# V of 24-bit precision in two float16 parts with a common power of two, and work moved between the vector engines, in a fused block-causal attention and gated convolution FFN

## The chip, the cores and the metric

The kernel runs on one core of a Trainium2 chip. Such a core has a matrix engine (TensorE, PE in the profile, with its weight loads shown apart as PEld), three engines for elementwise work (VectorE = DVE, ScalarE = ACT, GpSimd = POOL) and SyncE (SP), which here only starts data transfers. Each engine works through its own list of instructions in order and waits at semaphores for the others. [...]

The metric is the device time of one execution in microseconds (us).

## The reference

```python
# q, k, v: (8 batches, 8 heads, 576 positions, 64);  w_in (512, 1024), conv_w (3, 1024), w_out (1024, 512)
scores = scale * np.matmul(q, k.transpose(0, 1, 3, 2))          # scale = 1/8
scores = np.where(block_i >= block_j, scores, -1000000000.0)    # blocks of 64 positions
scores = scores - np.max(scores, axis=-1, keepdims=True)
attn = np.exp(scores)
attn = attn / (np.sum(attn, axis=-1, keepdims=True) + 1e-09)
attn_out = np.matmul(attn, v)
...
h = np.maximum(x @ w_in, 0.0)                                   # x: the heads side by side, (8, 576, 512)
conv_out = sum over k of conv_w[k] * h shifted by k - 1 along the sequence
out = (h * sigmoid(conv_out)) @ w_out
```

The weights arrive as float64 and are decoded on the chip. Everything is computed to nearly float32 precision: most factors are split into a high part and a low remainder, and each matrix product is made of three products (high x high, high x low, low x high).

## The kernel before

**Stages.** The work goes by pairs of heads; two heads of 64 channels fill the 128 partitions. The first batch (four pairs) is handled in two halves, A (positions 0 to 255) and B (the rest), with code of its own, so that the weights can be decoded beside it. The other 28 pairs go through `stage_t` (q and k are transposed on PE and split), `stage_s` (scores, mask, maximum, exponential, division, planes), a transposition of the planes, and `pair_pv`. After the fourth pair of a batch, `ffn` runs on its two halves. Its matrix products (L1887 into the hidden layer, L1953 out of it) are interleaved with the attention of the next batch.

**Planes.** Before the change `two_planes` splits each tile of normalized exponentials, scaled by 32768, into two float16 planes: the high one on GpSimd (L1366), the low one on VectorE (L1371). Query tile i (0 to 3) has 128 (i + 1) keys, and the last 64 queries (`last_s`) have 576, in two halves of 288. SP then issues one transposing transfer for each plane of each head (`xbar`, L1379, ten blocks of 128 x 128), and one more for the last queries' planes (`h` to `t`).

**V.** `load_v` splits V into three bfloat16 parts on GpSimd: copy, subtract, copy, subtract, each 640 wide. `pair_pv` then makes five products (parts 0, 1, 2 with the high plane, parts 0, 1 with the low one), in one burst for the queries 0 to 255 (4 multiplications a product) and one for the queries 256 to 575 (18 a product), all at L1844: 110 multiplications a pair.

**FFN.** For each chunk of 128 hidden channels `ffn` makes 12 multiplications into a PSUM bank (L1887), then a chain: rectify in place on ACT (L1901), middle tap on ACT into a buffer `t` (L1904), the two other taps on DVE (L1908, L1912), hyperbolic tangent on ACT (L1917), gate on DVE (L1920, the last reader of the bank), high part `gh` on ACT (L1924), low part `gl` on GpSimd (L1927). The output tiles are copied on ACT (L1961) and stored by SP (L1964).

**What sets the order.** Nothing is scheduled while the kernel runs. `Plan.order` lists every operation with an engine, an estimated duration and a target time from the table `TARGETS`, and lays the operations out engine by engine, by target among those whose inputs are ready by its estimates; it also hands out the PSUM banks. Where it expects PE to stand still it puts idle multiplications (`work`, L2078), which keep PE busy and give nothing. Each transfer takes the next of eight semaphores, and so waits until the transfer that used this semaphore last has landed (`DMAHW` in the rows below).

**The start.** `load_first` loads q and k of the first 256 positions of all heads in six pieces each, pairs 0, 1 and 2 to 3, into one buffer `qkt`; `first_t` transposes them pair by pair (L1319).

Of the kernel before, what the change touches and what calls it, by code (L numbers as in the profile page):

```python
# [349 lines left out]
class Plan:  # L350

    DRAIN = (0.165, 0.08, 0.1, 0.025, 0.0)
    SIGNAL = (0.04, 0.035, 0.035, 0.08, 0.1)
# [1758 lines left out]
```

## Time and profile before

| | before |
|---|---|
| median of 3 runs (lowest, highest) | 769.39 us (767.01, 769.42) |
| the profiled execution | 767.56 us |
| its span, first to last instruction | 765.6 us |
| busy: PE, DVE, ACT, POOL | 728.7, 634.3, 491.7, 447.5 us |
| mean granted clock of TensorE | 0.993 |

A row of a group reads: line, engine, operation, output <- inputs by the program's names, shape, count | busy time in us, mean ns of one | idle time of the engine just before them, and who ended it. In the timeline a row gives the start, the duration, the group, and in brackets the idle time before it and who ended it. Multiplications are pipelined, so their durations overlap, and the distance of the starts is what each costs. A row of waits reads: who waited <- for whom: us in total, times, longest us. SPq and ACTq are the queues of transfers that SP and ACT issue; issuing is not counted as busy time.

### The profile page before, as it was taken

Reading aid. Unit: us, or ns where it says so; the run is one execution under the profiler, and the core shown is the slowest. Engines: PE = TensorE matmul, PEld = TensorE weight load, DVE = VectorE, ACT = ScalarE, POOL = GpSimd, SP = SyncE. Lnnn points to the kernel's source line nnn. Section 1 sums busy time; section 2 is a strip of 40 time slices with the busy share of each in tenths; the row PEclk is TensorE's granted clock in tenths of the full one; section 3 lists DMA queues with packets and bytes.
Section 4 is the critical chain, followed back from the end, with each engine's and each line's share of the span. In section 5 each row is a group of like instructions: output and inputs, shape, how many; then the busy total and the mean of one; then the engine's idle time right before and its main releaser. Section 6 shows DMA issues by size and latency. Waiting matters only on the chain.

```text
span 765.6 us, 19659 instructions
## 1 busy us (share of the span) xinstructions
PE 728.7 (95%) x7028; PEld 617.5 (81%) x7028; DVE 634.3 (83%) x1749; ACT 491.7 (64%) x1466; POOL 447.5 (58%) x604
## 2 busy tenths in 40 slices
PE   5989999799999999999999999999989999999998
PEld 3656678686878879888988889788878888888987
DVE  0888899898999889899998888999878977996442
ACT  1788977655766648676765548576655746673654
POOL 0353476667667757475668655686745864673232
PEclk9999999999999999999999999999989999999999
DMA  5564446669858498376858468796749548665001
GB/s 155 139 191 117 110 108 131 118 128 179 166 101 172 92 161 161 86 162 136 155 93 176 98 136 144 126 181 116 151 86 154 126 98 157 123 115 87 29 28 42
DMA packets 323061, 96.35 MB, mean 126 GB/s; under 512 B 312316, under 2 KB 317460, under 8 KB 322964
## 3 DMA queue, kind: packets, MB, share of 16 engines
q1 hardware_dynamic: 322420, 94.97, 61.9%
q8 instruction: 56, 0.92, 0.5%
q14 instruction: 41, 0.34, 0.1%
q10 hardware_dynamic: 544, 0.13, 0.1%
HBM read 37.38 MB, written 9.44 MB: 61 GB/s over the span
## 4 chain that ended last, share of the span: by engine, by line
PE 60%; DVE 19%; DMA 8%; ACT 6%; issue 3%; POOL 1%; SPq 1%; ACTq 0%; POOLq 0%; DVEq 0%
PE bank L1953 21%; PE bank L1887 16%; PE bank L1844 10%; PE bank L1477 5%; DVE ptbl L1371 3%; DVE su L1493 3%; DMA t<-h 3%; PE bank L1400 2%; PE bank L1268 2%; DVE t L1908 2%; DVE t L1912 1%; DVE t L1920 1%; DMA ptbh<-ptbl 1%; DMA x<-in_moe_w_out_dram 1%; DVE su L1504 1%
## 5 line engine op out<-in xcount | busy, mean ns | idle before, releaser
L1887 PE MATMUL bank<-x,wih 128*128 128x290 f32 (+3 forms) x1024 | 193.5, 300 | 2.1 <-DVE t L1920 0.9
L1927 POOL TENSOR_TENSOR gl<-t,gh 128x289 fp32r<-128x289 f32 (+3 forms) x128 | 108.5, 855 | 107.6 <-ACT gh L1924 107.2
L1887 PEld LDWEIGHTS bank<-x,wih 128*128 128x128 f32 x1024 | 153.9, 188 | 10.1 <-issue 3.1
L1953 PE MATMUL bank<-woh,gh 128*128 128x512 f32 (+1 forms) x296 | 120.0, 406 | 1.0 <-POOL ptbl L1366 1.0
L1953 PE MATMUL bank<-wol,gh 128*128 128x512 f32 (+1 forms) x296 | 114.7, 388 | 0.0
L1953 PE MATMUL bank<-woh,gl 128*128 128x512 f32 (+1 forms) x296 | 114.6, 387 | 0.0
L1887 PE MATMUL bank<-x,wil 128*128 128x290 f32 (+3 forms) x512 | 109.8, 298 | 0.0
L1493 DVE TENSOR_REDUCE su<-bank 128x1 f32<-128x384 f32 (+2 forms) x224 | 100.5, 477 | 3.1 <-ACT p0f L1496 2.1
L1908 DVE SCALAR_TENSOR_TENSOR t<-bank,cw,t 128x289 f32<-128x289 f32 (+3 forms) x128 | 64.0, 506 | 29.9 <-ACT t L1904 29.5
L1887 PEld LDWEIGHTS bank<-x,wil 128*128 128x128 f32 x512 | 81.6, 188 | 2.4 <-issue 1.4
L1917 ACT ACTIVATE t<-t 128x289 f32<-128x289 f32 (+3 forms) x128 | 56.2, 444 | 25.3 <-DVE t L1912 24.8
L1901 ACT ACTIVATE bank<-bank 128x290 f32<-128x290 f32 (+3 forms) x128 | 51.1, 404 | 32.7 <-PE bank L1887 31.9
L1953 PEld LDWEIGHTS bank<-woh,gh 128*128 128x128 f32 x296 | 55.9, 189 | 15.6 <-issue 4.4
L1924 ACT ACTIVATE gh<-t 128x289 fp32r<-128x289 f32 (+3 forms) x128 | 55.0, 442 | 18.4 <-DVE t L1920 17.8
L1904 ACT ACTIVATE t<-bank,cw 128x289 f32<-128x289 f32 (+3 forms) x128 | 63.1, 499 | 4.1 <-POOL gl L1927 1.8
L1953 PEld LDWEIGHTS bank<-woh,gl 128*128 128x128 f32 x296 | 55.9, 189 | 11.9
L1912 DVE SCALAR_TENSOR_TENSOR t<-bank,cw,t 128x288 f32<-128x288 f32 (+3 forms) x128 | 63.5, 505 | 0.5
L1844 PEld LDWEIGHTS <-vx 128*64 128x64 bf16 x1540 | 52.7, 113 | 12.0 <-issue 11.1
L1953 PEld LDWEIGHTS bank<-wol,gh 128*128 128x128 f32 x296 | 56.0, 189 | 7.6
L1920 DVE SCALAR_TENSOR_TENSOR t<-t,bank 128x289 f32<-128x289 f32 (+3 forms) x128 | 56.1, 446 | 5.5 <-ACT t L1917 4.9
L1844 PEld LDWEIGHTS <-vv 128*64 128x64 bf16 x1540 | 50.5, 111 | 6.8 <-issue 6.7
L1844 PE MATMUL bank<-ptbx,vx 128*64 128x256 f16 (+1 forms) x840 | 53.5, 261 | 2.2 <-DMA ptbx<-ptbl 2.0
(189 smaller groups left out, 1757.5 us busy)
## 6 DMA issues: line engine op xcount, KB each, us to landing
out_dram<-stage SPq DMA_DIRECT2D x35, 256.0 KB, 2.5
vn<-in_v_dram SPq DMA_DIRECT2D x58, 128.0 KB, 2.5
...
```

The source lines that it names most:

```text
L1493: nc.vector.tensor_reduce(out=st.ap[:, k:k + 1], in_=sb.ap[:, cols(i)], op=ALU.max, axis=AX.X, negate=True)
L1844: nc.tensor.matmul(tb.ap[64 * j:64 * j + 64, c0:c1], vb.ap[:, j, c, w, :], x, start=first, stop=(w == 1 and z == 1 and c == jobs[-1][0]), ...
L1887: nc.tensor.matmul(fb.ap[:, 0:n2], wt[:, c, fs], xs[c][xi].ap[:, x0:x0 + n2], start=(n + c - c0 == 0), stop=(n + c - c0 == 3 * NCC - 1))
L1901: nc.scalar.activation(out=fb.ap[:, 0:n2], in_=fb.ap[:, 0:n2], func=AF.Relu, scale=0.5)
L1904: nc.scalar.activation(out=t.ap[:, 0:no], in_=fb.ap[:, own:own + no], func=AF.Copy, scale=cw[:, NFC + f:NFC + f + 1])
L1908: nc.vector.scalar_tensor_tensor(out=t.ap[:, i0:no], in0=fb.ap[:, own + i0 - 1:own + no - 1], scalar=cw[:, f:f + 1], in1=t.ap[:, i0:no], o ...
L1912: nc.vector.scalar_tensor_tensor(out=t.ap[:, 0:i1], in0=fb.ap[:, own + 1:own + 1 + i1], scalar=cw[:, 2 * NFC + f:2 * NFC + f + 1], in1=t.a ...
L1917: nc.scalar.activation(out=t.ap[:, 0:no], in_=t.ap[:, 0:no], func=AF.Tanh)
L1920: nc.vector.scalar_tensor_tensor(out=t.ap[:, 0:no], in0=t.ap[:, 0:no], scalar=1.0, in1=fb.ap[:, own:own + no], op0=ALU.add, op1=ALU.mult)
L1924: nc.scalar.activation(out=gbuf[0].ap[:, f, carry:carry + no], in_=t.ap[:, 0:no], func=AF.Copy)
L1927: nc.gpsimd.tensor_tensor(out=gbuf[1].ap[:, f, carry:carry + no], in0=t.ap[:, 0:no], in1=gbuf[0].ap[:, f, carry:carry + no], op=ALU.subtract)
L1953: nc.tensor.matmul(fb.ap[:, 0:cut], gbuf[a].ap[:, f, cs], w[:, f, ds], start=(f == 0 and n == 0), stop=(f == NFC - 1 and n == 2))
```

## The change

- **V.** Each pair's V is multiplied by a power of two so that it fits float16, and split in two float16 parts. ACT sums |V| along each row (a bound for its maximum), GpSimd puts the sums on a diagonal, one multiplication with a matrix of constants spreads them to all partitions, DVE takes the maximum and keeps its exponent bits. GpSimd scales V, copies the high part and subtracts for the low part. `pair_pv` makes three products (66 multiplications), and the copies out of PSUM undo the scale from a per-partition value.
- **Planes.** The planes of both heads lie together in one buffer of 40 blocks, in three pieces: query tiles 0 and 1 with both planes (12 blocks), high plane of tiles 2 and 3 (14), low plane (14). Three transfers take the place of four. The burst of queries 0 to 255 waits for the first piece alone. The 128-key tiles (i = 0) are split on GpSimd alone in three steps; the high planes of the 256-key tiles and of the last queries go to ACT.
- **Masks** are written by ACT instead of DVE. The 64 x 64 corner copies of q that SP made by transfers (L1304) are made by ACT and DVE from PSUM.
- **FFN**, in all batches but the first: the copy `gh` goes to GpSimd, and in chunks 1, 3, 5, 7 the third tap is a product on ACT and an addition on GpSimd.
- **Stores** are issued by ACT, except those of the last half.
- **The start.** `qkt` becomes six buffers, one for each of q and k and each piece.
- The planner counts 0.6 instead of 0.1 us of signalling for SP, some durations are changed, and the table of targets is new.

```diff
@@ planner, constants, first loads
-    SIGNAL = (0.04, 0.035, 0.035, 0.08, 0.1)
+    SIGNAL = (0.04, 0.035, 0.035, 0.08, 0.6)
...
-    HPOOL = (0, 1, 2, 3, 4)
+    HPOOL, HALL = (2, 3), (0,)
+    CPOOL = (1, 3, 5, 7)
+    MACT = True
+    NGRP = ((0, 1), (2,), (3, 4))
...
-    qkt = [nc.alloc_sbuf_tensor_at(f"qk{x}", [P, 2, 2, H, D], d, offset=at0).ap() for x, d in (("f", F32), ("r", F32R))]
+    FIRST = ((0, 1), (1, 2), (2, 4))
+    qkt = [[[nc.alloc_sbuf_tensor_at(f"qk{x}{z}{p0}", [P, 2, 2 * (p1 - p0), D], d, offset=at0 + 4 * D * H * 2 * z + 4 * D * 4 * p0).ap()
+             for p0, p1 in FIRST] for z in range(2)] for x, d in (("f", F32), ("r", F32R))]
@@ load_v
-        def copy(w):
+        def total():
+            nc.scalar.activation(out=piece(1).bitcast(BF16), in_=src(), func=AF.Abs, accum_out=sc.ap[:, 0:1])
+
+        def spread():
+            nc.gpsimd.tensor_scalar(out=dg.ap, in0=ident, scalar1=sc.ap[:, 0:1], scalar2=2.0 ** -100, op0=ALU.mult, op1=ALU.max)
+
+        def all_rows():
+            nc.tensor.matmul(tb.ap[:, 0:P], ones, dg.ap, start=True, stop=True)
+
+        def top():
+            nc.vector.tensor_reduce(out=sc.ap[:, 1:2], in_=tb.ap[:, 0:P], op=ALU.max, axis=AX.X)
+
+        def power(i):
...
-        def less():
-            nc.gpsimd.tensor_tensor(out=src(), in0=src(), in1=piece(0), op=ALU.subtract)
-
-        def last():
-            nc.gpsimd.tensor_tensor(out=piece(2), in0=src(), in1=piece(1), op=ALU.subtract)
+        def level():
+            nc.gpsimd.tensor_scalar(out=src(), in0=src(), scalar1=sc.ap[:, 2:3], scalar2=0.0, op0=ALU.mult, op1=ALU.add)
+
+        def high():
+            pool_copy(piece(0), src())
+
+        def low():
+            nc.gpsimd.tensor_tensor(out=piece(1), in0=src(), in1=piece(0), op=ALU.subtract)
@@ two_planes
+        def even():
+            nc.gpsimd.tensor_scalar(out=tb.ap, in0=tb.ap, scalar1=st.ap[:, col:col + 1], scalar2=0.0, op0=ALU.mult, op1=ALU.add)
+
+        def h1p():
+            pool_copy(hi(), c(tb.ap))
+
+        def h2p():
+            nc.gpsimd.tensor_tensor(out=lo(), in0=c(tb.ap), in1=hi(), op=ALU.subtract)
@@ stage_s
-                    nc.vector.memset(x, MASKED)
+                        if MACT:
+                            nc.scalar.activation(out=x, in_=maskt[0:64, :].unsqueeze(1).broadcast_to([64, len(tiles), 64]), func=AF.Copy)
@@ pair_pv
-                for w, z in ((0, 0), (1, 0), (2, 0), (0, 1), (1, 1)):
+                for w, z in ((0, 0), (1, 0), (0, 1)):
...
-            o = pl.op(PE, (0.77 if qa == 0 else 2.64, 0.05, 0.1), mm, at, deps=deps + [vdone] + (done4 if qa else []),
+            o = pl.op(PE, (0.47 if qa == 0 else 1.65, 0.05, 0.1), mm, at, deps=(deps[1:] + done4 if qa else deps[:1]) + vdone,
@@ ffn
+            def c2u(fb=fb, f=f, u=u):
+                nc.scalar.activation(out=u.ap[:, 0:i1], in_=fb.ap[:, own + 1:own + 1 + i1], func=AF.Copy,
+                                     scale=cw[:, 2 * NFC + f:2 * NFC + f + 1])
+
+            def c2p(t=t, u=u):
+                nc.gpsimd.tensor_tensor(out=t.ap[:, 0:i1], in0=t.ap[:, 0:i1], in1=u.ap[:, 0:i1], op=ALU.add)
...
+            def c5p(t=t, f=f):
+                pool_copy(gbuf[0].ap[:, f, carry:carry + no], t.ap[:, 0:no])
...
-                    nc.sync.dma_start(out=ofl[row:row + P, ds], in_=ob.ap[:, ds])
+                late_ = b == B - 1 and o1 == S
+
+                def st(ob=ob, row=row, ds=ds, eng=nc.sync if late_ else nc.scalar):
+                    eng.dma_start(out=ofl[row:row + P, ds], in_=ob.ap[:, ds])
```

Since the table of targets is new, the instructions stand in another order on every engine. Three places are shown. The first is SP's list at the start of the program, with what each transfer waits for (`qkf` is q and k of the first positions, `gh` and `gl` hold raw `w_in`, `ptbl` raw v). Before:

```order
L1004 DMA qkf<-in_q_dram 128x2x64 x2
L1194 DMA gh<-in_moe_w_in_dram 128x4x256
L1194 DMA gl<-in_moe_w_in_dram 128x4x256 [waits DMAHW0_49]
L1004 DMA qkf<-in_k_dram 128x2x64 [waits DMAHW1_49]
L1004 DMA qkf<-in_k_dram 128x2x64 [waits DMAHW2_49,PE_49]
L1194 DMA gh<-in_moe_w_in_dram 128x4x256 [waits DMAHW3_49]
L1004 DMA qkf<-in_k_dram 128x4x64 [waits DMAHW4_49]
```

And of the change:

```order
L1048 DMA qkf_117<-in_k_dram 128x2x64
L1238 DMA gh<-in_moe_w_in_dram 128x4x256
L1048 DMA qkf_117<-in_k_dram 128x2x64 [waits DMAHW0_49]
L1238 DMA gh<-in_moe_w_in_dram 128x4x256 [waits DMAHW1_49]
L1059 DMA ptbl<-in_v_dram 128x4x64 [waits DMAHW2_49]
L1048 DMA qkf_118<-in_k_dram 128x4x64 [waits DMAHW3_49]
```

The second piece of k for the second pair no longer waits for PE, and no later load of q or k there does.

The second place is TensorE's list at the same time (L1319 / L1370 transpose q and k of a pair, L1603 / L1684 are scores, L2078 / L2184 idle multiplications). Before:

```order
L2078 MATMUL bank<-blank 128x512 x8
L1319 MATMUL bank<-rident,qkr 128x128 x2
L2078 MATMUL bank<-rident 128x512 x5
...
L2078 MATMUL bank<-rident 128x512 x2
L1603 MATMUL bank<-kh,qh 128x128 x2
...
L2078 MATMUL bank<-rident 128x512 x13
...
L1150 MATMUL bank<-wih,nident 128x512
```

And of the change:

```order
L2184 MATMUL bank<-blank 128x512 x10
L1370 MATMUL bank<-rident,qkr_119 128x128 x2
L2184 MATMUL bank<-rident 128x512 x2
L1370 MATMUL bank<-rident,qkr_122 128x128 x2
L1370 MATMUL bank<-rident,qkr_120 128x128 x2
L1684 MATMUL bank<-kh,qh 128x128 x2
...
L2184 MATMUL bank<-rident 128x512 x3
L1370 MATMUL bank<-rident,qkr_123 128x128 x2
L2184 MATMUL bank<-rident 128x512 x5
```

The 13 idle multiplications ahead of the last transpose of the second pair are 5 now, and smaller groups stand further on, 45 in all at the start instead of 37.

The third place is TensorE's list in the first batch after the start, around the first bursts of attention times V (L1477 / L1537 are scores, L1400 / L1464 scores of the last 64 queries, L1887 / L1970 the FFN). Before:

```order
L1844 MATMUL bank<-ptbx,vx 64x128
L1400 MATMUL bank<-kh,qdh_150 128x288
...
L1400 MATMUL bank<-kl,qdh_150 128x288
L1887 MATMUL bank<-x,wih 128x322 x2
L1887 MATMUL bank<-x,wil 128x322 x2
L1268 MATMUL bank<-rident,qnr_110 128x128 x5
L1268 MATMUL bank<-rident,knr_112 128x128
```

And of the change:

```order
L1464 MATMUL bank<-kl,qdh_163 128x288
L2184 MATMUL bank<-rident 128x512 x7
L1537 MATMUL bank<-kh,qh 128x128 x2
...
L1537 MATMUL bank<-kh,qh 128x256 x2
...
L2184 MATMUL bank<-rident 128x512
L1537 MATMUL bank<-kh,qh 128x384 x2
...
L2184 MATMUL bank<-rident 128x512 x6
```

Between the scores of a pair there are now idle multiplications, 19 in this batch (none before), and 35 in all after the start (2 before).

More of the change, by code (lines that the diff above doesn't have):

```diff
@@ L825 @@
     cw = cp.tile([P, KC * NFC], F32, tag="cw", name="cw")
+    unit = cp.tile([P, 9], F32, tag="unit", name="unit")
+    nc.vector.memset(unit, 1.0 / PSC)
+    ones = cp.tile([P, P], F32R, tag="ones", name="ones")
+    nc.scalar.activation(out=ones, in_=ident, func=AF.Copy, scale=0.0, bias=2.0 ** -13)
     blank = cp.tile([P, P], F32R, tag="blank", name="blank")
@@ L881, in vhead @@
         return b
+    scales = Buf(cp, [P, 4, 8], F32, "vs")
     vnw = Buf(cp, [P, 5, 2, D], F32, "vn")
@@ L919, in load_v @@
         n = len(pl.tags.get("vb", ()))
-        vb = follow("vb", Buf(cp, [P, 2, 5, 3, D], BF16, ("vx", "vv")[n % 2]), ("vv0", "vv1") if n == 1 else (), 2)
+        vb = follow("vb", Buf(cp, [P, 2, 5, 2, D], F16, ("vx", "vv")[n % 2]), ("vv0", "vv1") if n == 1 else (), 2)
+        sc = pl.buf(cp, None, None, "vs", 4, part=(scales, n % 4))
+        dg = one([P, P], F32R, "dg")
+        tb = bank("tv")
         ops = [ld]
@@ L946, in load_v @@
-        n = 10 * D
-        o = pl.op(POOL, c_pool(n), copy(0), at + 5, deps=ops, bufs=[vn, vb])
-        o = pl.op(POOL, c_pool(n, True), less, at + 5.5, deps=[o], bufs=[vn, vb])
-        o = pl.op(POOL, c_pool(n), copy(1), at + 7, deps=[o], bufs=[vn, vb])
-        o = pl.op(POOL, c_pool(n, True), last, at + 7.5, deps=[o], bufs=[vn, vb])
-        return vb, o
+                x = sc.ap.bitcast(I32)
+                nc.vector.tensor_scalar(out=x[:, i + 1:i + 2], in0=x[:, i:i + 1], scalar1=0x7F800000, scalar2=0x7F800000,
+                                        op0=ALU.bitwise_and, op1=ALU.bitwise_xor)
@@ new lines, in power @@
+            return go
+        def level():
[4 more added lines that the diff above has]
+            nc.gpsimd.tensor_tensor(out=piece(1), in0=src(), in1=piece(0), op=ALU.subtract)
+        o = pl.op(ACT, 0.72, total, at + 3.6, deps=ops, bufs=[vn, vb, sc])
+        o = pl.op(POOL, 0.3, spread, at + 4, deps=[o], bufs=[sc, dg])
+        o = pl.op(PE, run(mm_(P)), all_rows, at + 4.5, deps=[o], bufs=[dg, tb])
@@ L953, in follow @@
+        o = pl.op(DVE, 0.25, top, at + 5, deps=[o], bufs=[tb, sc])
+        o = pl.op(DVE, 0.09, power(1), at + 5, deps=[o], bufs=[sc])
+        o1 = pl.op(DVE, 0.09, power(2), at + 5, deps=[o], bufs=[sc])
+        o = pl.op(POOL, 0.8, level, at + 5.5, deps=[o], bufs=[vn, sc])
+        o = pl.op(POOL, 0.8, high, at + 6, deps=[o], bufs=[vn, vb])
+        o = pl.op(POOL, 1.44, low, at + 7, deps=[o], bufs=[vn, vb])
+        return (vb, sc), [o, o1]
     def follow(tag, b, olds, cap=1):
@@ L976, in late, with plane @@
         return b
-    planes = Buf(cp, [P, 2, 2, 10, P], F16, "ptbl")
-    turned = [Buf(cp, [P, 2, 2, 10, P], F16, nm) for nm in ("ptbx", "ptbh")]
-    def plane(hh):
-        return follow(f"plane{hh}", Part(planes, hh), ("ptb10", "ptb11"))
+    planes = Buf(cp, [P, 40, P], F16, "ptbl")
+    turned = [Buf(cp, [P, 40, P], F16, nm) for nm in ("ptbx", "ptbh")]
+    pieces = ((0, 12), (12, 26), (26, 40))
+    def plane():
+        return [follow(f"plane{z}", Part(planes, slice(a, b)), ("ptb10", "ptb11")) for z, (a, b) in enumerate(pieces)]
     lasts = {x: Buf(cp, [P, 2, 5 * P], F16, x) for x in ("h4", "t4")}
@@ L987, in last_plane, with turn @@
         return follow(x, Part(lasts[x], slice(0, 2)), ())
-    def turn(hh):
-        n = len(pl.tags.get(f"turn{hh}", ()))
-        return follow(f"turn{hh}", Part(turned[n % 2], hh), ("ptb00", "ptb01") if n == 1 else (), 2)
+    def turn():
+        n = len(pl.tags.get("turn0", ()))
+        return [follow(f"turn{z}", Part(turned[n % 2], slice(a, b)), ("ptb00", "ptb01") if n == 1 else (), 2)
+                for z, (a, b) in enumerate(pieces)]
     def load_first():
@@ L1289, in naturals, with co_hi, co_lo @@
                 es[w].append(pl.op(DVE, c_dve(n, two_in=True), ev_lo, t0 + 0.7, deps=[e], bufs=[tb, hi, lo]))
+            if corner and len(outs) == 2:
+                hi, lo, zs = corner
+                for r in (slice(0, 64), slice(64, P)):
+                    def co_hi(tb=tb, r=r, hi=hi):
+                        nc.scalar.activation(out=hi.ap[r, r], in_=tb.ap[r, P:P + 64], func=AF.Copy, scale=SCALE)
+                    def co_lo(tb=tb, r=r, hi=hi, lo=lo):
+                        nc.vector.scalar_tensor_tensor(out=lo.ap[r, r], in0=tb.ap[r, P:P + 64], scalar=SCALE, in1=hi.ap[r, r],
+                                                       op0=ALU.mult, op1=ALU.subtract)
+                    e = pl.op(ACT, c_act(64) + 0.03, co_hi, t0 + 0.3, deps=[o] + zs, bufs=[tb, hi])
+                    es[2].append(e)
+                    es[2].append(pl.op(DVE, c_dve(64, two_in=True), co_lo, t0 + 0.7, deps=[e] + zs, bufs=[tb, hi, lo]))
         return es
@@ L1507, in i2 @@
             def i2(a=a, b_=b_):
-                nc.vector.reciprocal(st.ap[:, 16 + a:16 + b_], st.ap[:, 16 + a:16 + b_])
-            o = pl.op(DVE, 0.075, i1, t0 + 1.2 + OSH, deps=es, bufs=[st])
-            o = pl.op(DVE, 0.09, i2, t0 + 1.2 + OSH, deps=[o], bufs=[st])
-            for hh, sb in enumerate(sbs):
-                for i in tiles:
-                    def part(w, i=i, pn=pn[hh]):
-                        return lambda: pn.ap[:, w, first_block[i]:first_block[i] + 2 * i + 1:2, :]
-                    h = two_planes(es_[hh][i], lambda y: y.rearrange("p (c n) -> p c n", n=P), 128 * i + 128, st,
-                                   16 + 2 * i + hh, part(0), part(1), pn[hh], t0 + 1.5 + OSH + 0.5 * hh, [o], i in HPOOL)
-                    for w in range(2):
-                        hs[hh][w].append(h[w])
@@ L1521, in stage_s @@
-        bars = [xbar(lambda w=w, hh=hh: pn[hh].ap[:, w].rearrange("p c n -> p (c n)"), lambda w=w, hh=hh: tn[hh].ap[:, w],
-                     at + OXB_ + 0.5 * w + 0.8 * hh, hs[hh][w], [pn[hh], tn[hh]]) for hh in range(2) for w in range(2)]
-        return tn, bars, last_s(t, ready4, at + OST * 3)
+                nc.vector.reciprocal(st.ap[:, 24 + a:24 + b_], st.ap[:, 24 + a:24 + b_])
+            t0 = at + OST * g[-1] - (OST if g[-1] == 4 else 0) + 1.2 + OSH
+            o = pl.op(DVE, 0.19, i1, t0, deps=[e for k in g for e in exps[k]], bufs=[st])
@@ new lines, in stage_s, with part @@
+            o = pl.op(DVE, 0.09, i2, t0, deps=[o], bufs=[st])
+            for k in g:
+                norms[k] = o
+        for i in range(4):
+            for hh in range(2):
+                own = pn[0:1] if i < 2 else pn[1:3]
+                def part(w, i=i, own=own, hh=hh):
+                    x = own[0 if i < 2 else w]
+                    b = 6 * hh + 3 * w + 1 - i if i < 2 else 7 * hh + 3 - i
+                    return lambda: x.ap[:, b:b + 2 * i + 1:2, :]
+                h = two_planes(es_[hh][i], lambda y: y.rearrange("p (c n) -> p c n", n=P), 128 * i + 128, st,
+                               24 + 2 * i + hh, part(0), part(1), own, at + OST * max(i - 1, 0) + 1.5 + OSH + 0.5 * hh, [norms[i]], 2 * (i in HALL) or i in HPOOL)
+                for w in range(2):
+                    hs[0 if i < 2 else 1 + w].append(h[w])
@@ L1526, in stage_sb @@
+        bars = [xbar(lambda x=pn[z]: x.ap.rearrange("p c n -> p (c n)"), lambda x=tn[z]: x.ap,
+                     at + OXB_ - 3.0 * (z == 0) + 0.5 * (z == 2), hs[z], [pn[z], tn[z]], (12, 14, 14)[z]) for z in range(3)]
+        return tn, bars, p4[1]([norms[4]], 32)
     def stage_sb(ops, at):
@@ L1897, in ffn @@
             t = pl.buf(pt3, [P, S - Q1 + 1], F32, "t", 3)
+            u = None
+            if b and f in CPOOL:
+                z = len(pl.tags.get("u", ()))
+                u = follow("u", Buf(cp, [P, 384], F32, ("ptah", "ptal")[z % 2]), ("ptah", "ptal") if z < 2 else (), 2)
             def relu(fb=fb):
-                nc.scalar.activation(out=fb.ap[:, 0:n2], in_=fb.ap[:, 0:n2], func=AF.Relu, scale=0.5)
+                nc.scalar.activation(out=fb.ap[:, 0:n2], in_=fb.ap[:, 0:n2], func=AF.Relu, scale=0.5 if b == 0 else 2.0 ** -17)
             def c1(fb=fb, t=t, f=f):
```

195 lines of the change are left out of this document (106 added, 89 removed), and 497 rows, old and new, of the table TARGETS.

## The prediction

> **What bounds the kernel now.** I read the page first, its totals and its chain of what ended last, and then the stages one by one.
>
> ```profile
> span 765.6 us, 19659 instructions
> PE 728.7 (95%) x7028; PEld 617.5 (81%) x7028; DVE 634.3 (83%) x1749; ACT 491.7 (64%) x1466; POOL 447.5 (58%) x604
> PE 60%; DVE 19%; DMA 8%; ACT 6%; issue 3%; POOL 1%; SPq 1%; ACTq 0%; POOLq 0%; DVEq 0%
> ```
>
> TensorE is busy for 95% of the span and holds 60% of the chain; VectorE, next, holds 19%. The profiled execution took 767.56 us, 2 us more than its span and 1.8 below the median of 769.39; the sum below starts from 767.6. The table of stretches (busy us of PE, weight loads, DVE, ACT, POOL, then granted clock) says where PE is not full:
>
> ```profile
> 0.00:50.00 50.00, 38.61 (x187) 25.79 (x189) 28.19 (x86) 28.82 (x87) 14.76 (x33) 1.00 0.61 165
> 50.00:100.00 50.00, 47.66 (x300) 33.69 (x300) 44.43 (x113) 41.76 (x118) 21.57 (x31) 1.00 0.43 114
> 350.00:400.00 50.00, 49.98 (x494) 43.19 (x493) 47.62 (x139) 33.98 (x110) 30.84 (x41) 1.00 0.65 128
> ```
>
> In the middle PE stands still for 0.02 us of 50, so a TensorE instruction taken away there shortens the run by its own time, as long as nobody takes PE's place; VectorE at 47.6 of 50 is the candidate. The first stretch has 11.4 of the 36.9 us of PE's idleness, and its own limit, shown in part (2).
>
> **The change, part by part.** *(1) Three products for five in attention times V.* The timeline of TensorE shows one pair of heads whose 110 multiplications at L1844 ran without a wait (start, duration, then the group):
>
> ```profile
> 380.03 0.37 PE L1268 MATMUL bank<-rident,knr 128*128 128x128 f32 x3
> 380.34 1.40 PE L1844 MATMUL bank<-ptbx,vx 128*64 128x256 f16 x28
> 381.72 0.55 PE L1844 MATMUL bank<-ptbx,vx 128*64 128x256 f16 x8
> 382.27 0.55 PE L1844 MATMUL bank<-ptbx,vx 128*64 128x256 f16 x8
> 383.99 0.53 PE L1887 MATMUL bank<-x,wih 128*128 128x288 f32 x2
> ```
>
> The durations overlap, so I take starts. From 381.72 to 382.27 is one product over the later 320 queries, 0.54 us over three such steps. The five of them take 2.7; the other 20 multiplications, for the first 256 queries, take the remaining 0.84 (from 380.34 to 381.18), 0.17 per product. Two products are dropped, 2 x (0.54 + 0.17) = 1.42 us a pair. There are 28 such pairs (3080 multiplications become 1848): **-39.6 us**. All of it lies in stretches where PE is full. Weight loads fall with it, 1232 of them.
>
> Added on PE is one multiplication of 128 columns a pair (L961 of the new kernel), which spreads the row sums of |V|. The trace has none alone; three transposes of that width took 0.31 from 380.03 to the next start, so 0.07 each in a run and 0.31 at most with the change of weights. I take 0.15, nearer to the run since weights load ahead: 28 x 0.15 = **+4.2** (2 to 9).
>
> *(2) The start.* The first q and k rows now lie in six buffers where before they were one. PE, and SP's queue:
>
> ```profile
> 9.96 0.47 PE L1319 MATMUL bank<-rident,qkr 128*128 128x128 f32 x2 [5.13 <-DMA qkf<-in_k_dram]
> 18.47 5.32 PE L2078 MATMUL bank<-rident 128*128 128x512 f32 x13
> 23.63 0.29 PE L1319 MATMUL bank<-rident,qkr 128*128 128x128 f32 x2
> 2.26 1.03 SPq L1004 DMA_DIRECT2D qkf<-in_q_dram  x2
> 4.39 8.91 SPq L1004 DMA_DIRECT2D qkf<-in_k_dram  x2
> 13.86 0.51 SPq L1004 DMA_DIRECT2D qkf<-in_k_dram  x1
> SPq L1004 <- PE bank L1319: 15.9, 3, 7.9
> ```
>
> SP's second load of k stood 7.9 us in the queue until PE had read what was already in the tile, and 15.9 in three such waits. So k of the second pair of heads was turned at 23.63, and PE filled 18.47 to 23.63 with 13 idle multiplications. In the new order no load of q or k waits for PE. The load of k then goes out at about 4.7 instead of 12.9, lands some 3 us later, and the transposes stand at 9 to 11: 13 us sooner. How much reaches the end? DVE, with 44.4 of 50 busy in the second stretch, must follow, and the order now holds 25 idle multiplications between the second pair's scores and the first FFN work or shortly before it, where 9 stood; 16 x 0.24 = 4 us are given back. That leaves 9, of which I take **-8**; 0 if weight decoding sets this stage, 13 if nothing does.
>
> *(3) Idle multiplications later on.* They stand where a gap is expected, and cost PE their own time. Of them 35 now lie after the start, 2 did before.
>
> ```profile
> 399.87 0.40 PE L1953 MATMUL bank<-woh,gh 128*128 128x512 f32 x1
> 400.11 0.39 PE L1953 MATMUL bank<-wol,gh 128*128 128x512 f32 x1
> ```
>
> 512 columns go every 0.24 us, so 33 more make **+7.6**, or nothing if PE would have stood there anyway (19 of them lie in the first batch after the start, where it did).
>
> *(4) Work moved between the other engines.* Rows of the groups (busy total, mean ns):
>
> ```profile
> L1912 DVE SCALAR_TENSOR_TENSOR t<-bank,cw,t 128x288 f32<-128x288 f32 (+3 forms) x128 | 63.5, 505 | 0.5
> L1486 DVE MEMSET bank<- 64x64 f32 (+1 forms) x168 | 20.1, 130 | 14.9 <-PE bank L1477 13.9
> L1371 DVE SCALAR_TENSOR_TENSOR ptbl<-p0f,su,ptbl 128x128 f16<-128x128 f32 x56 | 29.0, 521 | 1.5 <-DMA ptbh<-ptbl 1.3
> L1924 ACT ACTIVATE gh<-t 128x289 fp32r<-128x289 f32 (+3 forms) x128 | 55.0, 442 | 18.4 <-DVE t L1920 17.8 <-DVE st L1411 0.2 <-POOL gh L834 0.2
> L1904 ACT ACTIVATE t<-bank,cw 128x289 f32<-128x289 f32 (+3 forms) x128 | 63.1, 499 | 4.1 <-POOL gl L1927 1.8
> L839 ACT ACTIVATE ptbh<-bank 64x128 f32<-64x128 f32 x8 | 2.2, 270 | 0.7 <-PE bank L1690 0.6
> L1927 POOL TENSOR_TENSOR gl<-t,gh 128x289 fp32r<-128x289 f32 (+3 forms) x128 | 108.5, 855 | 107.6 <-ACT gh L1924 107.2
> L1366 POOL TENSOR_SCALAR h<-p4f,st 128x288 f16<-128x288 f32 x56 | 33.8, 610 | 15.1 <-ACT stage L1961 6.4 <-DVE st L1434 4.6 <-ACT p2f L1496 2.0
> L1366 POOL TENSOR_SCALAR ptbl<-p0f,su 128x128 f16<-128x128 f32 x56 | 23.6, 424 | 30.4 <-DVE su L1508 18.9 <-ACT p2f L1496 4.3 <-ACT t L1917 3.4
> L834 POOL TENSOR_SCALAR vx<-vn 128x640 bf16<-128x640 f32 x28 | 22.8, 816 | 18.5 <-PE bank L1844 8.9 <-PE bank L1887 5.0 <-DMA vn<-in_v_dram 4.1
> L941 POOL TENSOR_TENSOR vn<-vn,vx 128x640 f32<-128x640 f32 x14 | 20.4, 1454 | 0.7
> ```
>
> VectorE loses the masks (20.1), 56 taps (56 x 0.505 = 28.3) and the 128-key low planes (29.0), and some 10 in small steps. It gets about 140 small operations (corner copies, maximum and powers of V) of 0.13, as the masks, to 0.5: 28 at 0.2. So 634 - 87 + 28 = 575 us. ScalarE loses 112 copies (49.5) and gets 168 masks and 56 corner copies (0.27 each, 60), two sets of 56 planes and 56 tap products (0.50 each, 84), 28 sums of |V| (0.9 each, 25): 612 us, and 33 store issues at 0.51 as on SP, 17 more. GpSimd takes 3.5 us for V's four steps of a pair (0.8 twice, 1.5 and a narrow 0.4) where two copies and two subtractions took 4.5, 28 less in all, and loses the 256- and 288-wide high planes (56 at between 0.42 and 0.61, and 33.8: 62); it gets 112 copies (0.61 each, 68), 56 tap sums (0.855 each, 48) and the 128-key planes in three steps of 0.43 for one of 0.42 (48): about 520 us. Of some 732, that is 79% for DVE, 86% for ACT with its issues and 71% for POOL, all below PE's 94%, and no worse than DVE's 83% before. So I cost these moves at **0**, covered by PE's work; without that cover the two that lengthen the FFN's chain cost most, see the slow rival.
>
> The stores leave SP's queue, where one waiting for its data held what came behind it, transposes among them:
>
> ```profile
> SPq L1964 <- ACT stage L1961: 45.4, 9, 16.0
> PE bank L1844 <- DMA t<-h: 5.8, 7, 1.9
> ```
>
> PE waited 5.8 us in all for the plane transposes, so less in that queue is worth 0 to 6; on ACT a store waits for a semaphore that an earlier transfer must release, and what stands behind it there are masks and exponentials that free score banks. The trace has no store on ACT: between a gain of 6 and 33 x 1.9 = 63 lost, if each held PE like the longest of those waits. ACT writes the data itself just before, so I take 0.
>
> The sum: 767.6 - 39.6 + 4.2 - 8 + 7.6 = **732 us**.
>
> **The rivals.** *PE's waits grow.* With 1.4 us less work a pair there is less to do while a transpose is under way. The price is seen where it happened:
>
> ```profile
> 140.00:145.00 5.00, 4.83 (x74) 4.59 (x70) 1.71 (x6) 1.74 (x5) 2.06 (x2) 0.75 0.72 138
> 138.66 0.35 PE L1844 MATMUL bank<-t,vx 128*64 128x64 f16 x10 [1.90 <-DMA t<-h]
> 139.68 0.93 PE L1844 MATMUL bank<-ptbx,vx 128*64 128x256 f16 x7
> 140.69 0.94 PE L1844 MATMUL bank<-ptbx,vx 128*64 128x256 f16 x7
> ```
>
> After a wait of 1.9 us the granted clock fell to 0.75 over five microseconds, and a product took 1.01 instead of 0.54. If a pair waits 0.7 us longer on the mean, partly for the clock, it is 28 x 0.7 = 20: 752 us. For it: the planes now need three transposes of all rows, the first of which feeds the first 256 queries. Against it: that first one no longer waits for the planes of the 384- and 512-key tiles. [...]
>
> *Slower: the taps on GpSimd hold the FFN's banks.* In half of the chunks of seven batches, 56, the second tap is 0.855 on POOL instead of 0.505 on DVE, and first waits in POOL's queue behind steps of up to 1.5. L1920's product, the last reader of the bank, comes later by that. If a queue of 1 us is added to the 0.35 and PE waits for all of it at L1887, it is 56 x 1.35 = 76, 808 us; from 0.64 us a chunk on (36 / 56) the kernel is no faster than before. For it: POOL goes from 58 to 71%. Against: it sat idle 107 us ahead of L1927, and PE has other work between chunks. [...]
>
> *The start gives nothing* because decoding the weights sets that stage: 740. *Fewer waits than before:* stores out of SP's queue (-6) and planned gaps that fall where PE stood anyway (-5): 721.
>
> **How the numbers follow.** The forecast, 724 to 744 with the start's rival in it, has 0.65 (0.50 and 0.15). Growing waits, around 752, have 0.18; fewer waits, around 721, 0.11; the slow one 0.06. The range 718 to 754 leaves out the slow rival (0.06), what of growing waits lies beyond 754 (0.07) and what of fewer waits lies under 718 (0.04). A measurement of this kernel cannot tell less than 0.3% (2.3 us) from no change. Only the slow rival, where most of it lies beyond 772, and the far end of growing waits (0.02) reach 767: faster 0.92, the same 0.03, slower 0.05.
>
> **What would show it.** In the new profile: a pair's 66 multiplications in about 2.2 us; the second pair's k turned near 10 us, not 23.6; PE's own busy time near 690; DVE near 575, ACT near 610, POOL near 520. Wrong would be: PE waiting at the FFN's first product for the product of the gate, or for a score bank behind a store on ACT; VectorE above 90% of a shorter span; a granted clock below 0.98.

## The result, and the profile after

| | before | after |
|---|---|---|
| median (lowest, highest), 4 runs each | 769.40 us (767.01, 769.68) | 727.89 us (726.76, 729.15) |
| ratio, 95% interval | | 0.9467 [0.9443, 0.9492] |
| span of the profiled execution | 765.6 us | 727.4 us |
| PE busy, PE idle | 728.7, 36.9 us | 705.6, 21.8 us |
| granted clock | 0.993 | 0.995 |

The kernel became 41.5 us faster; 732 was forecast, in a range of 718 to 754. The page of the new kernel, its totals and its chain:

```profile
span 727.4 us, 17504 instructions
PE 705.6 (97%) x5865; PEld 583.4 (80%) x5865; DVE 602.7 (83%) x1554; ACT 574.0 (79%) x1803; POOL 510.6 (70%) x772
PE 63%; DVE 16%; ACT 14%; issue 3%; POOL 3%; DMA 0%; ACTq 0%; DVEq 0%; POOLq 0%
```

PE's busy time fell by 23.1 us and its idle time by 15.1; together that is the 38.2 by which the span fell. Transfers, 8% of the chain before, are gone from it, and ScalarE went from 6% to 14%. The timeline of the start, on PE and then in SP's queue:

```profile
5.77 0.49 PE L1370 MATMUL bank<-rident,qkr 128*128 128x128 f32 x2
8.57 0.97 PE L2184 MATMUL bank<-rident 128*128 128x512 f32 x3
9.60 0.36 PE L1370 MATMUL bank<-rident,qkr 128*128 128x128 f32 x2
11.29 0.49 PE L1684 MATMUL bank<-kh,qh 64*128 64x128 f32 x4
```

```profile
3.79 0.51 SPq L1048 DMA_DIRECT2D qkf<-in_k_dram  x1
5.40 0.87 SPq L1048 DMA_DIRECT2D qkf<-in_k_dram  x1
```

The second pair's k is turned at 9.60 (23.63 before), and no load of k stands in the queue. On PE's timeline a pair's later burst of attention times V:

```profile
391.82 0.57 PE L1927 MATMUL bank<-ptbh,vv 128*64 128x256 f16 x8
392.38 0.55 PE L1927 MATMUL bank<-ptbh,vv 128*64 128x256 f16 x8
392.92 0.55 PE L1927 MATMUL bank<-ptbh,vv 128*64 128x256 f16 x8
393.56 0.44 PE L1537 MATMUL bank<-kh,qh 64*128 64x384 f32 x2
```

Three products, 0.56 and 0.54 us apart by their starts, stand where five stood. The table of stretches, with its columns as before:

```profile
0.00:50.00 50.00, 45.98 (x262) 30.96 (x262) 38.34 (x111) 37.54 (x112) 19.15 (x38) 1.00 0.68 188
100.00:150.00 50.00, 46.44 (x357) 37.46 (x357) 43.32 (x120) 42.00 (x135) 29.55 (x44) 1.00 0.62 125
150.00:200.00 50.00, 46.53 (x478) 37.58 (x476) 42.69 (x114) 38.79 (x132) 32.48 (x50) 0.93 0.85 166
350.00:400.00 50.00, 48.23 (x453) 41.16 (x450) 43.22 (x109) 41.22 (x133) 40.41 (x58) 1.00 0.82 142
```

The first 50 us hold 46.0 us of PE's work instead of 38.6. Between 100 and 200 us PE still stands idle 7 us.

The later runs lie on other chips, where the kernel before took 764.4 to 765.4 us and the new one 727.4 (ratio 0.9511 [0.9479, 0.9543]). Since that differs from 0.9467 by 0.0044, or 3.4 us, prices across chips are good to about that, and are given as differences of ratios times 765 us, against 0.9511.

### The profile page after: what moved, and what is told of

Its sections match the earlier page's. It is cut to its first block, busy times and chain, and to the rows that moved or that the text cites. A ratio compares the mean times of both kernels' runs of the same rounds, so it can differ in the third digit from the quotient of the medians.

```text
span 727.4 us, 17504 instructions
## 1 busy us (share of the span) xinstructions
PE 705.6 (97%) x5865; PEld 583.4 (80%) x5865; DVE 602.7 (83%) x1554; ACT 574.0 (79%) x1803; POOL 510.6 (70%) x772
## 4 chain that ended last, share of the span: by engine, by line
PE 63%; DVE 16%; ACT 14%; issue 3%; POOL 3%; DMA 0%; ACTq 0%; DVEq 0%; POOLq 0%
PE bank L2056 22%; PE bank L1970 18%; PE bank L1537 6%; PE bank L1927 6%; DVE ptbl L1422 3%; PE bank L1865 3%; DVE su L1559 3%; PE bank L1464 2%; PE bank L1312 2%; PE bank L2184 2%; DVE t L1994 2%; ACT t L1990 1%; ACT bank L1987 1%; ACT p1f L1562 1%; ACT p2f L1562 1%
## 5 line engine op out<-in xcount | busy, mean ns | idle before, releaser
L1970 PE MATMUL bank<-x,wih 128*128 128x290 f32 (+3 forms) x1024 | 195.1, 301 | 2.2 <-DVE x L1938 0.7
L1970 PEld LDWEIGHTS bank<-x,wih 128*128 128x128 f32 x1024 | 154.4, 188 | 12.2 <-issue 2.8
L1970 PE MATMUL bank<-x,wil 128*128 128x290 f32 (+3 forms) x512 | 110.3, 298 | 0.0
L1559 DVE TENSOR_REDUCE su<-bank 128x1 f32<-128x128 f32 (+2 forms) x224 | 101.1, 481 | 10.0 <-ACT bank L1550 6.2
L1994 DVE SCALAR_TENSOR_TENSOR t<-bank,cw,t 128x286 f32<-128x286 f32 (+3 forms) x128 | 65.1, 513 | 29.1 <-ACT t L1990 23.0
L1970 PEld LDWEIGHTS bank<-x,wil 128*128 128x128 f32 x512 | 81.9, 188 | 1.2
L1990 ACT ACTIVATE t<-bank,cw 128x287 f32<-128x287 f32 (+3 forms) x128 | 63.4, 501 | 8.1 <-POOL gl L2023 6.6
L850 POOL TENSOR_SCALAR gh<-t 128x287 fp32r<-128x287 f32 (+1 forms) x112 | 53.7, 483 | 22.7 <-DVE t L2013 19.7
L2013 DVE SCALAR_TENSOR_TENSOR t<-t,bank 128x287 f32<-128x287 f32 (+3 forms) x128 | 56.6, 448 | 12.5 <-ACT t L2010 11.1
L2010 ACT ACTIVATE t<-t 128x287 f32<-128x287 f32 (+3 forms) x128 | 57.0, 446 | 12.0 <-POOL t L2007 5.9
L1417 POOL TENSOR_SCALAR ptbl<-p3f,su 128x512 f16<-128x512 f32 x56 | 43.1, 775 | 18.8 <-DVE su L1582 18.0
L1550 ACT ACTIVATE bank<-maskt 64x128 f32<-64x128 f32 (+1 forms) x168 | 35.1, 232 | 17.5 <-PE bank L1537 16.3
L1422 DVE SCALAR_TENSOR_TENSOR ptbl<-p3f,su,ptbl 128x512 f16<-128x512 f32 x56 | 49.0, 876 | 0.0
L1562 ACT ACTIVATE p3f<-bank,su 128x512 f32<-128x512 f32 x56 | 38.3, 687 | 9.4 <-DVE su L1559 5.8
```

The costliest lines, as they stand in the source:

```text
L850: nc.gpsimd.tensor_scalar(out=dst, in0=src, scalar1=1.0, scalar2=0.0, op0=ALU.mult, op1=ALU.add)
L1422: nc.vector.scalar_tensor_tensor(out=lo(), in0=c(tb.ap), scalar=st.ap[:, col:col + 1], in1=hi(), op0=ALU.mult, op1=ALU.subtract)
L1559: nc.vector.tensor_reduce(out=st.ap[:, k:k + 1], in_=sb.ap[:, cols(i)], op=ALU.max, axis=AX.X, negate=True)
L1562: nc.scalar.activation(out=x.ap, in_=sb.ap[:, cols(i)], func=AF.Exp, bias=st.ap[:, k:k + 1], accum_out=st.ap[:, 8 + k:9 + k])
L1970: nc.tensor.matmul(fb.ap[:, 0:n2], wt[:, c, fs], xs[c][xi].ap[:, x0:x0 + n2], start=(n + c - c0 == 0), stop=(n + c - c0 == 3 * NCC - 1))
L1990: nc.scalar.activation(out=t.ap[:, 0:no], in_=fb.ap[:, own:own + no], func=AF.Copy, scale=cw[:, NFC + f:NFC + f + 1])
```

## The experiments

**Three products alone.** In the kernel before:

```diff
-for w, z in ((0, 0), (1, 0), (2, 0), (0, 1), (1, 1)):
+for w, z in ((0, 0), (1, 0), (0, 1)):
...
```

> The kernel before with three products of attention times V instead of five, nothing else moved; the two products left out are the third part of V by the high plane and the second part by the low plane, so its output lacks these small terms. Theory (a TensorE instruction taken away shortens the run by its own time): 28 x 1.42 = 39.6 us, about 730. Rival (another engine or a transfer takes PE's place): from the first of the 28 pairs to the last the new kernel gained only 18.6 us on the old (567.2 against 548.6 between the ends of their bursts), so some 20 to 30 us, 740 to 750, with PE's idle time up by the rest of the 39.6.

Measured: 750.83 us against 764.82, ratio 0.9829 [0.9800, 0.9858]: 13 to 14 us less. A third of the 39.6 arrived. The page and its chain:

```profile
span 750.0 us, 17195 instructions
PE 696.2 (93%) x5796; PEld 579.8 (77%) x5796; DVE 638.6 (85%) x1749; ACT 490.9 (65%) x1466; POOL 447.5 (60%) x604
PE 41%; DVE 35%; ACT 9%; DMA 7%; issue 5%; POOL 2%; SPq 1%; ACTq 0%; POOLq 0%; DVEq 0%
```

The two worst stretches, and PE's two longest rows of waits:

```profile
150.00:200.00 50.00, 45.23 (x433) 35.58 (x431) 49.10 (x136) 29.52 (x93) 35.91 (x48) 1.00 0.84 156
200.00:250.00 50.00, 43.99 (x435) 38.25 (x436) 46.74 (x128) 33.65 (x99) 35.38 (x48) 0.97 0.73 141
```

```profile
PE bank L1844 <- DMA t<-h: 5.8, 9, 2.2
PE bank L1844 <- DMA ptbx<-ptbl: 5.2, 6, 2.0
```

PE's idle time rose from 36.9 to 53.8 us, and its busy time fell by 32.5 instead of 39.6, the clock granted being 0.981. VectorE's share of the chain went from 19 to 35%: it is busy for 49.1 of 50 us in one stretch. The rows of PE's waits add up to 12.0 us for VectorE (3.6 before) and 12.4 for ScalarE (7.0 before); those for transposing transfers grew less, from 8.1 to 11.0. So the rival is right here: as soon as PE has less to do, the others take its place.

**Two moves in place, in the old order.** Three products, and the masks and the 128-key low planes taken from VectorE:

```diff
-nc.vector.memset(x, MASKED)
+nc.scalar.activation(out=x, in_=maskt[0:64, :]..., func=AF.Copy)
...
 def h2():
+    if n == P:
+        nc.gpsimd.tensor_scalar(out=tb.ap, in0=tb.ap, scalar1=..., scalar2=0.0, op0=ALU.mult, op1=ALU.add)
+        nc.gpsimd.tensor_tensor(out=lo(), in0=c(tb.ap), in1=hi(), op=ALU.subtract)
+        return
```

> The kernel before with three products (the run above with 14 us less than the kernel before) and with two of the change's moves put in place, in the old order: the 168 masks written by ScalarE (VectorE loses 20 us) and the 56 low planes of 128 keys made by GpSimd in two steps (VectorE loses 29). It leaves out the same two products. Theory A (VectorE at 85% is what kept 25 us of the products' 39.6): at least 10 us less than with three products alone, so 24 or more less than the kernel before. Theory B (the order of PE's instructions, planned for five products, is what kept them: PE comes to instructions whose planes or transposes are not there yet): within 4 us of three products alone.

Measured: 757.38 against 765.43, ratio 0.9887 [0.9833, 0.9941]: 8 us less than before, 4 more than three products alone by the ratios, with intervals that overlap. VectorE's busy time fell from 638.6 to 612.8 us, by 25.8 where 49 were meant, and no time came of it:

```profile
L1497 DVE TENSOR_REDUCE su<-bank 128x1 f32<-128x384 f32 (+2 forms) x224 | 101.5, 482 | 34.5 <-ACT bank L1490 29.9 <-ACT p0f L1500 2.9 <-ACT p1f L1500 0.8
L1375 DVE SCALAR_TENSOR_TENSOR ptbl<-p2f,su,ptbl 128x384 f16<-128x384 f32 x56 | 45.3, 811 | 7.8 <-POOL ptbl L1366 6.6 <-DMA ptbx<-ptbl 1.3
```

VectorE's maximum now waits 29.9 us for the masks on ScalarE, which stand in an order not made for them (in the new kernel it waits 6.2 for them). So theory A has no support here, though it is not refuted cleanly: the relief came out at half its size, and the moves brought a wait of their own.

**The order laid anew for three products.** The planner is told the shorter bursts, its due times stay:

```diff
-o = pl.op(PE, (0.77 if qa == 0 else 2.64, 0.05, 0.1), mm, at, ...
+o = pl.op(PE, (0.47 if qa == 0 else 1.65, 0.05, 0.1), mm, at, ...
```

> The kernel before with three products, and with the planner told so (a pair's two bursts at 0.47 and 1.65 us instead of 0.77 and 2.64), so that it lays the order of all engines out anew from the same due times; no work is moved between engines. It leaves out the same two products. Theory A (VectorE keeps the gain): within 4 us of three products alone, 14 less than the kernel before. Theory B (the stale order keeps it): 10 us or more less than three products alone.

Measured: 770.29 against 765.43, ratio 1.0054 [1.0023, 1.0085]. Theory B's number fell too, by far: all that the products had brought is lost, and 4 us more. Among PE's longest waits are now those for loads, for the FFN's gate product and for exponentials (L1496):

```profile
PE bank L1268 <- DMA qnf<-in_k_dram: 8.7, 2, 6.0
PE bank L1887 <- DVE t L1920: 3.4, 3, 2.0
PE bank L1887 <- ACT p3f L1496: 3.2, 3, 2.0
```

Two orders with three products each differ by some 17 us (0.9829 and 1.0054); 19 idle multiplications, which the planner put into the second, are some 5 of them at 0.24. So an order alone can be worth over a quarter of the whole change. New durations with the old due times make a worse order here, not a better one.

**Five products in the new kernel.** The reverse of the first:

```diff
-for w, z in ((0, 0), (1, 0), (0, 1)):
+for w, z in ((0, 0), (1, 0), (1, 1), (1, 1), (0, 1)):
...
```

> The new kernel with five products in each pair's burst: the product of both low parts is added twice (two more than the new kernel's three, of the same shapes). Theory (PE sets the end through all 28 pairs): 39.6 us more, about 767. Rival (in some of the pairs other work sets the pace, or the added products fill PE's waits, of which 21.8 us are left): 20 to 32 us more, 748 to 760.

Measured: 759.54, ratio 0.9947 [0.9921, 0.9973], 33 us more than the new kernel (37 against its first ratio).

```profile
span 758.8 us, 19968 instructions
PE 742.7 (98%) x7097; PEld 622.4 (82%) x7097; DVE 602.9 (79%) x1554; ACT 578.1 (76%) x1803; POOL 507.9 (67%) x772
PE 83%; DVE 7%; ACT 6%; issue 2%; POOL 1%; ACTq 0%; POOLq 0%
```

PE's busy time rose by 37.1 and its idle time fell from 21.8 to 16.1. With PE at 83% of the chain, nearly all of an added instruction reaches the end; in the new order the two products are worth 33 to 37 us, and 13 in the old one.

**The start, from both sides.** The buffers alone in the kernel before, and one buffer again in the new kernel:

```diff
-qkt = [nc.alloc_sbuf_tensor_at(f"qk{x}", [P, 2, 2, H, D], d, offset=at0).ap() ...]
+qkt = [[[nc.alloc_sbuf_tensor_at(f"qk{x}{z}{p0}", [P, 2, 2 * (p1 - p0), D], d, ...).ap()
+         for p0, p1 in FIRST] for z in range(2)] ...]
...
```

> The kernel before with its first q and k rows in six buffers, nothing else moved: the idle multiplications of the start stay where they were. Theory of the prediction: 8 us less (761), 13 at most (756); since the 13 idle multiplications ahead of the second pair's k still run, perhaps only the two waits for k in front of them, 2.3 and up to 5.1, are saved (762 to 767). Rival (decoding the weights sets this stage): 769, no change.

> The new kernel with the first q and k rows in one buffer again, as before, so that SP's loads wait for PE's reads; nothing else moved. Theory of the prediction: 8 us more, about 736 (13 at most, 741). Rival 1 (all that the first pair gained comes from here): its burst of attention times V stood 16.6 us sooner in the new kernel, so 16 more, 744. Rival 2 (decoding the weights sets this stage): no change, 728.

Measured: the buffers alone 754.15, ratio 0.9873 [0.9844, 0.9901], 10 us less than before; one buffer again 735.91, ratio 0.9635 [0.9609, 0.9662], 9.5 us more than the new kernel (13 against its first ratio). PE of both, the kernel before with six buffers first:

```profile
9.33 0.37 PE L1321 MATMUL bank<-rident,qkr 128*128 128x128 f32 x2
9.53 3.21 PE L2080 MATMUL bank<-rident 128*128 128x512 f32 x13
12.58 0.29 PE L1321 MATMUL bank<-rident,qkr 128*128 128x128 f32 x2
```

```profile
7.61 0.34 PE L1370 MATMUL bank<-rident,qkr 128*128 128x128 f32 x2 [1.90 <-issue]
10.96 0.72 PE L1370 MATMUL bank<-rident,qkr 128*128 128x128 f32 x4 [2.48 <-DMA qkf<-in_k_dram]
16.38 0.47 PE L1370 MATMUL bank<-rident,qkr 128*128 128x128 f32 x2 [0.98 <-DMA qkf<-in_q_dram]
```

The second pair's k comes at 12.58 instead of 23.63 even with the 13 idle multiplications ahead of it. The forecast of 8, up to 13, holds; that decoding the weights sets this stage does not.

**Two moves undone in the new kernel.**

```diff
-nc.scalar.activation(out=x, in_=maskt[0:64, :]..., func=AF.Copy)
+nc.vector.memset(x, MASKED)
...
-nc.gpsimd.tensor_tensor(out=t..., in0=t..., in1=u..., op=ALU.add)
+nc.vector.scalar_tensor_tensor(out=t..., in0=fb..., scalar=cw..., in1=t..., op0=ALU.mult, op1=ALU.add)
```

> The new kernel with two of the moves undone at the places where they stand: the 168 masks written by VectorE, and the 56 second taps multiplied and added by VectorE from the bank in one step (without ScalarE's 56 copies). VectorE gets some 48 us more (651 of about 730, 89%). Theory of the prediction (the moves are covered by PE either way): no change within 4 us of the new kernel. Rival, after three products alone gave 14 us of 39.6 in the old order with VectorE at up to 49.1 of 50 us: VectorE's relief is what lets PE's saving reach the end, so 12 to 25 us more than the new kernel.

 

The new kernel itself ran beside it:

> The new kernel unchanged, as the measure for the runs of this call: by the first ratio 0.9467 of the kernel before, so 724 where the kernel before takes 765.

Measured: 732.82 against the new kernel's 727.43 on the same chip, 5.4 us more (ratios 0.9576 [0.9543, 0.9609] and 0.9511). Between both theories: the moves are worth something, not 12 to 25. VectorE's busy time rose by 24.8 us, not 48. The new kernel's steps first, then those with the moves undone:

```profile
L1994 DVE SCALAR_TENSOR_TENSOR t<-bank,cw,t 128x286 f32<-128x286 f32 (+3 forms) x128 | 65.1, 512 | 29.2 <-ACT t L1990 23.0 <-ACT ptah L2003 3.9 <-ACT ptal L2003 1.4
L1422 DVE SCALAR_TENSOR_TENSOR ptbl<-p1f,su,ptbl 128x256 f16<-128x256 f32 x56 | 33.2, 599 | 0.9 <-ACT ptbl L1419 0.9
L1422 DVE SCALAR_TENSOR_TENSOR h<-p4f,su,h 128x288 f16<-128x288 f32 x56 | 37.4, 673 | 2.1 <-ACT h L1419 1.9
```

```profile
L1991 DVE SCALAR_TENSOR_TENSOR t<-bank,cw,t 128x286 f32<-128x286 f32 (+3 forms) x128 | 64.1, 504 | 19.9 <-ACT t L1987 19.1
L1422 DVE SCALAR_TENSOR_TENSOR ptbl<-p1f,su,ptbl 128x256 f16<-128x256 f32 x56 | 29.8, 536 | 0.8 <-ACT ptbl L1419 0.6
L1422 DVE SCALAR_TENSOR_TENSOR h<-p4f,su,h 128x288 f16<-128x288 f32 x56 | 35.5, 638 | 1.7 <-ACT h L1419 1.4
```

With GpSimd's load at 463.7 us instead of 510.0, VectorE's low planes, both inputs in SBUF, became 5 and 11% shorter; its taps, one input in PSUM (the banks that PE writes), only 2%. Of the 23 us between 48 and 24.8, some 15 are such growth: the rows of the steps that stayed are longer in the new kernel by that much, 11 of it in steps with two inputs in SBUF. The rest comes from counting rows: a step's row overlaps the next by some 0.05 us on the mean, so VectorE's rows add up to 723.4 and 689.9 us where its busy times are 627.6 and 602.8, and a row taken away takes less than its length off the busy time.

**Without the late idle multiplications.**

```diff
+late = len(fills) > 11
 def go():
+    if late:
+        return
```

> The new kernel without its 35 idle multiplications after the start. Theory of the prediction (they cost PE their own time, 0.24 each): 8 us less than the new kernel. Rival 1 (PE would stand there anyway, at least at the 21 between 137 and 190 us, where PE has 46.5 busy of 50): no change within 3 us. Rival 2 (they keep the clock up, 0.93 granted between 150 and 200 us even with them): 2 to 6 us more.

Measured: 728.75 against 727.43, ratio 0.9519 [0.9488, 0.9550]: 1.3 us more, no difference that can be told. PE between 150 and 200 us without them, and with them (the new kernel, run beside it):

```profile
150.00:200.00 50.00, 43.90 (x476) 36.41 (x475) 44.05 (x119) 40.60 (x138) 33.00 (x51) 0.93 0.87 171
```

```profile
150.00:200.00 50.00, 45.99 (x463) 37.45 (x460) 43.89 (x120) 40.57 (x136) 33.75 (x52) 1.00 0.90 170
```

PE stands still longer in this stretch, at a granted clock of 0.93 instead of 1.00. Over the span its busy time fell by 3.4 and its idle time rose by 5.8. On balance they cost nothing. Why is open in part: 35 of them at 0.24 make 8.4 us, not 3.4, and the granted clock was 0.986 to 0.993 in the four runs without them, 0.995 to 1.000 in all eight of the new kernel. So the second rival, that they keep the clock up, is not refuted; the mean clocks differ by 0.7%, which on PE's 703 us is an estimated 5 us.

**Without V's maximum, and without its scale.** First `total`, `spread`, `all_rows` and `power` do nothing and `top` writes constants, then `level` is left out as well:

```diff
-nc.vector.tensor_reduce(out=sc.ap[:, 1:2], in_=tb.ap[:, 0:P], op=ALU.max, axis=AX.X)
+nc.vector.memset(sc.ap[:, 2:3], 32.0)
+nc.vector.memset(sc.ap[:, 3:4], 2.0 / 32.0)
```

> The new kernel without V's maximum: the sums of |V| on ScalarE, the diagonal on GpSimd, the multiplication that spreads it to all rows, VectorE's maximum and powers are left out, and two constants (32 and 1/16) stand in the places of the scales. Theory of the prediction (28 multiplications of 0.15 on PE, the rest covered): 4 us less than the new kernel. Rival (the chain through four engines also holds others: ScalarE loses 28 x 0.93 = 26 us and GpSimd 22): 8 us or more less.

> The new kernel without V's maximum, as in the run that left the chain out (5 us less than the new kernel), and without the multiplication by the scale on GpSimd as well (28 x 0.85 = 24 us of its 490). Theory (GpSimd is covered by PE): no change against that run, 5 us less than the new kernel. Rival (V's planes come late behind GpSimd's queue): 3 us or more less than that run.

Measured: 722.47 without the maximum, 5.0 us less than the new kernel on the same chip (0.9439 [0.9410, 0.9468] and 0.9511); 720.32 without the scale too, ratio 0.9400 [0.9350, 0.9449], not told from the run before it. PE's busy time fell by 4.3 us with the chain (702.8 to 698.5), its idle time by 1.0: the chain through four engines costs about what its step on PE costs, and 24 us of GpSimd's work next to nothing. Both beat both kernels, but only since V's range is taken as known.

**Stores from SP again.** `eng=nc.sync` for all of them.

> The new kernel with all stores issued from SP's queue again, in the same order. Theory of the prediction (0 taken, 0 to 6 us possible): within 2 us of the new kernel. Rival (PE waited 5.8 us for the planes' transposes behind SP's stores before, and for none of them in the new kernel): 4 to 8 us more.

Measured: 727.15, ratio 0.9492 [0.9437, 0.9546], as the new kernel. The waits of SP's queue, of the new kernel (whose last half's stores are SP's) and then with all stores on SP:

```profile
SPq L2069 <- ACT stage L2064: 57.3, 3, 53.0
```

```profile
SPq L2069 <- ACT stage L2064: 67.6, 13, 29.1
```

More stores stand in that queue, but the rows of PE's waits add up to 17.0 us against 16.6: nothing on PE came later for it.

## Why the prediction was right, and where it was not

**The time** was right, 727.9 for 732. Its steps, one by one:

*(1) Two products less.* The count and the 0.54 of a step were right. The step that failed is the premise that a TensorE instruction taken away "shortens the run by its own time, as long as nobody takes PE's place". It was read from the stretch 350 to 400 us, the fullest but one; the mean over the stretches was 47.8 of 50. In the old order two thirds of the 39.6 did not arrive: PE's idle time grew by 16.9 us, mostly in waits for VectorE and ScalarE, and its busy time fell by 7.1 less than the count, at a granted clock of 0.981 instead of 0.993. In the new order they are worth 33 to 37, so the term is 3 to 7 too large. The multiplication over all rows was put at 4.2; the whole chain costs 5.0.

*(2) The start*, -8 forecast: 9.5 to 13 in the new order and 10 in the old. The mechanism (SP's load held back until PE had read the shared buffer) is shown from both sides.

*(3) Late idle multiplications*, +7.6 forecast: nothing. The prediction named one reason, that PE would stand there anyway, as the lower bound, and took the upper; of the 35, 21 lie between 137 and 190 us, where PE lacks 3.5 us in 50. A second possible one, the clock, was not in the sum.

*(4) Moves at 0*: two of them are worth 5.4 us. The busy times were 602.7, 574.0 and 510.6 for the 575, 612 and 520 forecast. The working added and subtracted totals of rows, which overlap: before the change VectorE's rows add up to 733.0 us and ScalarE's to 601.1, against 634.3 and 491.7 busy. By rows VectorE lost 43.3 of the 59 forecast and ScalarE gained 112.5 of 120, while their busy times moved by 31.6 and 82.3. VectorE's small steps were also too cheap at 28 us; four of their rows alone make 39.5:

```profile
L1341 DVE SCALAR_TENSOR_TENSOR qdl<-bank,qdh 64x64 fp32r<-64x64 f32 x56 | 12.2, 218 | 4.1 <-ACT qh L1325 1.9 <-ACT qdh L1338 1.2 <-ACT kh L1325 0.4
L1492 DVE TENSOR_TENSOR su<-st 128x1 f32<-128x1 f32 x28 | 11.4, 406 | 4.3 <-ACT p4f L1480 4.1
L969 DVE TENSOR_SCALAR vs<-vs 128x1 int32<-128x1 int32 x56 | 8.0, 143 | 0.1
L964 DVE TENSOR_REDUCE vs<-bank 128x1 f32<-128x128 f32 x28 | 7.9, 282 | 1.7 <-PE bank L961 1.6
```

ScalarE's masks took 232 ns instead of 270 and its 64-wide copies 215. *Stores at 0*: right.

So 732 came out well partly by luck. The saving by the products was put 3 to 7 us too high, which made the forecast too fast. Idle multiplications that cost nothing stood at 7.6, moves that save 5 at 0, and the start's saving 1.5 to 5 too low; these made it too slow, and the two sides cancelled in part.

**The rivals.** *PE's waits grow* (752) did not happen in the new kernel: its waits for transfers fell from 16.5 to 2.2 us, and none is for a transposing one (in the other profiled execution of this kernel one is, of 0.9). The old order with three products does show growing waits, at about the price given (17 us of idle time and 7 of PE's own busy time, for 20), but not by the mechanism named: waits for transposing transfers grew by 2.9 us, those for VectorE and ScalarE by 13.8. Whether transposes in three pieces, as the prediction argued, or the new due times prevented it in the new kernel was not tried. *The taps on GpSimd* (808) would have shown at the FFN's products:

```profile
PE bank L2056 <- DVE t L2013: 0.7, 1, 0.7
PE bank L1970 <- DVE t L2013: 0.6, 2, 0.3
```

That, with one wait of 1.1 us ahead of q's transposes, is all PE waits for the gate's product; GpSimd's taps took 859 to 867 ns, as forecast. On VectorE, with the moves undone, the same 56 take 504, so the step is 1.7 times as long on GpSimd, and yet undoing it, together with the masks, cost 5.4 us. *Fewer waits* (721) is in part what happened, 15.1 us less idle time, 7.4 of it in the first 50 us; but the stores, which it named, had no part in it.

**What stays open.** Three products (13 to 14 us) and the buffers (10) make 24 in the old order; the change gave 37 on those chips with V's chain, which costs 5, in it. If the two add up, which was not run, some 18 us belong to the order as a whole: new due times, transposes in three pieces, corner copies without transfers, the moves. The single prices taken from the new kernel do not add up to the whole either (33, 9.5 and 5.4, less 5, make 43), perhaps since an order made for one set of instructions makes each undone part look dear. Due times could not be tried apart: a table belongs to one list of operations.
